# A fused sparse-attention, Fourier-mixing and MLP kernel whose step list is issued in another order on all five engines

## The chip, the cores and the metric

The kernel runs on one NeuronCore of a Trainium2 chip. The metric is device time in microseconds (us) of one execution. Three runs of the kernel before gave 300.67, 300.26 and 299.35 us, a median of 300.26. The profile is of one execution, whose span from its first to its last instruction is 297.65 us.

Five engines have a queue of instructions each and start them strictly in the order of that queue: TensorE (PE, matrix multiplies; its weight loads are shown as PEld), VectorE (DVE), ScalarE (ACT), GpSimd (POOL) and SyncE (SP, which only issues transfers). An instruction that needs another engine's result waits on a semaphore, and everything behind it in its own queue waits with it.

## The reference

Four batches of 768 positions, eight heads of 64. Attention keeps, for every query, its own block of 64 keys and the best three earlier blocks by a gate; its output is x (768 x 512 per batch). Then a two-dimensional Fourier transform is added to x, the rows are normalised, and an MLP of width 2048 follows.

```python
k_rep = k.reshape(B, H, n_blocks, block, D).mean(axis=3)
gate_scores = np.einsum('bhsd,bhnd->bhsn', q, k_rep)      # causal blocks only
top_idx = np.argsort(gate_scores, axis=-1)[..., -3:]      # and the query's own block
scores = scale * np.matmul(q, k.transpose(0, 1, 3, 2))    # masked by block and causally
x = softmax(scores) @ v                                   # heads side by side: (B, 768, 512)
u = x + np.real(np.fft.fft(np.fft.fft(x, axis=1), axis=2))
un = (u - mean(u)) / np.sqrt(var(u) + 1e-06)
out = u + np.maximum(un @ w_ch1, 0.0) @ w_ch2
```

## The kernel before

The work is cut into steps of one to 42 instructions. A string, ORDER, lists every step once, and a loop at the end of the kernel calls the steps in that order. Each engine gets its instructions in exactly this order; no scheduler moves anything. What an instruction must wait for is worked out from the order too: it waits for whatever it reads, and for earlier readers of what it overwrites. Two rules of that bookkeeping matter here. First, waits are kept by tile, so that a write to one half of a tile waits for an earlier-listed read of the other half. Second, two engines that read the same PSUM tile do so one after the other, in the listed order.

The heads are taken in 16 pairs P, four to a batch b. The steps, by their names in ORDER:

- `Lk`, `Lq`, `Lv`: SP issues the loads of k, q, v of a pair. `tk`, `tq`: six TensorE transposes each (line 289). `ks`: VectorE sums the transposed k by blocks (294), `kh` scales the sums (222). `kc`: ScalarE copies k (305; two instructions on line 308 from pair 7 on). `qc`: q to SBUF (316), `qs`: GpSimd converts it (225).
- `g`: gate scores on TensorE (335, 342). `gt`, `gx`, `gl`, `gm`: VectorE transposes them, finds each row's third best, compares, transposes back (349 to 389). `K`, from pair 7 on: GpSimd puts the mask below the q rows (395, 225), so that the score matmul adds it; before pair 7 the mask is added by matmuls (424).
- `s`: one of six score tiles of a pair (412, 417). `e`: its exponential on ScalarE (434). `d`: GpSimd clears above the diagonal (440). `vc`: v is converted. `v`: 42 matmuls with v (452). `x`: VectorE divides by the row sums (463, 222), which also frees the PSUM tile.
- `fs`, `fd`, `f`: VectorE folds x by the transform's symmetries (222). `y`: first transform, two halves per batch (522, 528); `tr` (VectorE, 541) and `ty` (ScalarE, 535) both read the PSUM tile of a half. `m`: second transform (555, 556); `u`: adds x (569, 575); `xu`: shifts the rows (581); `xt` and `un`: transpose, for batch 0 by TensorE (588, 593), later by DMA (596).
- `bn`, `nv`, `nr`: variance and its root. `W`: GpSimd issues the load of a chunk of w1: hidden tiles 0 to 3, 4 to 9, 10 to 15. `X`: half of w2. `w:b,it`: one hidden tile, eight matmuls (632, 634); `r`: its relu, on VectorE for every fourth tile (642), else on ScalarE (644). `c:b,st,h`: eight matmuls of the second product for rows st, half h of the hidden tiles (659; the last rows in column halves, 651). `o`: VectorE scales c and adds u (671). `od`: SP stores the rows.

PSUM holds four tiles of two banks each. All TensorE results pass through these four, so that a new one waits until an earlier tile has been read for the last time. Two row groups st share one c tile, one bank each:

```python
g = next(x for x in (W2_LAST if b == B - 1 else W2_SETS) if st in x)
if st == g[0] and h == 0:
    c_ps[b, g[0]] = pst([128, len(g), 512], f"c{st}_{b}")
```

with W2_SETS = ((0, 1), (2, 3), (4, 5)) and W2_LAST = ((0, 1), (2, 3), (4,), (5,)). Then `c:0,4,*` and `c:0,5,*` write the two halves of one tile, and `o:0,4` and `o:0,5` read one half each.

Of the kernel before, what the change touches and what calls it, by code (L numbers as in the profile page):

```python
# [117 lines left out]
tk:4 gl:2,1 e:1,2 d:1,3 gm:2 g:3 d:1,4 ks:4 d:1,0 v:0 d:1,5 gt:3 vc:1 kc:4 gx:3 e:1,1 s:2,5 Lv:3
Lq:6 LF:0 Lq:7 Lk:6 Lk:7 LT:0 s:2,3 kh:4 gl:3,0 e:2,5 gl:3,1 s:2,4 e:2,3 d:1,1 x:0 tq:5 qs:4 e:2,4
g:4 d:2,3 gm:3 qc:5 s:2,0 d:2,4 s:2,2 d:1,2 e:2,0 gt:4 d:2,5 tk:5 vc:2 gx:4 e:2,2 s:2,1 ks:5 d:2,0  # L120
Lv:4 Lq:8 Lk:8 s:3,1 e:2,1 v:1 gl:4,0 kh:5 gl:4,1 kc:5 d:2,1 gm:4 d:2,2 s:3,2 x:1 e:3,1 vc:3 g:5
e:3,2 Lv:5 Lc:0 d:3,1 s:3,5 gt:5 s:3,0 fs:0,1 e:3,5 s:3,3 d:3,2 gx:5 e:3,0 s:3,4 fs:1,1 tq:6
gl:5,0 e:3,3 fs:0,0 v:2 gl:5,1 fs:1,0 e:3,4 d:3,3 qc:6 d:3,0 s:4,5 x:2 d:3,4 s:4,4 e:4,5 d:3,5
# [664 lines left out]
```

## Time and profile before

| What | us |
|---|---|
| three runs | 300.67, 300.26, 299.35 |
| median | 300.26 |
| profiled execution, first to last instruction | 297.65 |
| first score tile's exponential starts | 13.38 |
| first W1 tile's first matmul | 60.32 |
| last matmul starts its step | 291.93 |

The page of the profile gives busy time by engine, the span in 40 slices, the chain of work that ended last, and the costliest groups of instructions. Its lines number the kernel before. A group's line reads: line, engine, operation, what it writes and reads with shapes, how many, then busy time in us and mean ns of one, then how long the engine had been idle before them and what ended that. The clock that TensorE was granted stands at 1.00 in the whole execution.

### The profile page before, as it was taken

The page shows a single profiled execution, that of the slowest core. Times are in us where ns is not written, and L with a number is a line of the kernel's source. Part 1 is how long each engine was busy: PE and PEld are TensorE (multiplying, and loading weights), DVE is VectorE, ACT ScalarE, POOL GpSimd, SP SyncE. Part 2 cuts the span into 40 slices and gives each one's busy share as a digit, 9 for nine tenths or more (in the row PEclk, how much of TensorE's full clock was granted, in tenths as well). Part 3 has the DMA queues.
Part 4 walks back from the last instruction along what each step waited for, and adds up shares of the span by engine and source line. Part 5 has one row for each costly group of instructions (what it writes and reads, how often), then busy time and mean ns, then how long its engine had stood idle before and what let it go on. Part 6 is the DMA issues. An engine that isn't in the chain of part 4 may idle for free.

```text
...
## 1 busy us (share of the span) xinstructions
PE 285.7 (96%) x2633; PEld 179.1 (60%) x2633; DVE 189.2 (64%) x604; ACT 164.8 (55%) x207; POOL 111.0 (37%) x286
## 2 busy tenths in 40 slices
PE   7798999999999999999999999999999999999994
...
GB/s 170 216 204 220 237 228 202 200 212 206 209 195 214 213 58 174 119 168 178 1 2 2 0 1 143 37 72 70 3 0 2 35 97 47 141 0 2 0 94 121
DMA packets 92768, 33.45 MB, mean 112 GB/s; under 512 B 85504, under 2 KB 89536, under 8 KB 92736
## 3 DMA queue, kind: packets, MB, share of 16 engines
...
q10 hardware_dynamic: 1712, 0.40, 0.7%
...
HBM read 28.55 MB, written 6.29 MB: 117 GB/s over the span
## 4 chain that ended last, share of the span: by engine, by line
PE 79%; DMA 6%; SPq 4%; ACT 4%; issue 3%; POOL 2%; DVE 1%; ACTq 0%; DVEq 0%; POOLq 0%
PE c L659 26%; PE h L632 19%; PE h L634 9%; PE sc L417 7%; PE av L452 5%; PE tp L289 4%; SPq L272 4%; DMA w<-in_moe_w_ch_dram 3%; ACT pt L434 3%; PE yp L522 2%; DMA nat<-in_q_dram 2%; PE mx L556 1%; PE mx L555 1%; PE g L342 1%; PE c L651 1%
## 5 line engine op out<-in xcount | busy, mean ns | idle before, releaser
L434 ACT ACTIVATE pt<-sc 128x1024 f16<-128x1024 f32 (+1 forms) x96 | 83.2, 925 | 25.7 <-PE sc L417 19.5
L632 PE MATMUL h<-unT,w 128*128 128x512 f16 x256 | 85.1, 379 | 0.4 <-DMA w<-in_moe_w_ch_dram 0.4
L659 PE MATMUL c<-w_sb,hT 128*128 128x512 f16 x368 | 83.8, 379 | 0.0
L634 PE MATMUL h<-unT,w 128*128 128x256 f16 x256 | 69.7, 272 | 0.1
L644 ACT ACTIVATE hT<-h 128x768 f16<-128x768 f32 x48 | 37.8, 813 | 44.2 <-PE h L634 44.1
L659 PEld LDWEIGHTS <-hT 128*128 128x128 f16 x368 | 35.6, 98 | 39.3 <-issue 0.5
L440 POOL TENSOR_SCALAR_AFFINE_SELECT pt<-pt 128x256 f16<-128x256 f16 x96 | 37.3, 411 | 54.7 <-ACT pt L434 53.7
L632 PEld LDWEIGHTS <-w 128*128 128x128 f16 x256 | 24.9, 97 | 29.1 <-issue 0.7
L671 DVE SCALAR_TENSOR_TENSOR u<-c,rs,u 128x512 f32<-128x512 f32 (+1 forms) x25 | 17.6, 726 | 31.2 <-PE c L659 30.4
L642 DVE TENSOR_SCALAR hT<-h 128x768 f16<-128x768 f32 x16 | 15.3, 954 | 30.2 <-PE h L634 30.2
L289 PE MATMUL tp<-id,nat 128*128 128x128 f32 x192 | 26.8, 278 | 4.3 <-DVE lt L380 1.0
L581 ACT ACTIVATE x<-u,nm 128x512 f16<-128x512 f32 x24 | 15.9, 715 | 22.4 <-DVE nm L575 22.3
L634 PEld LDWEIGHTS <-w 128*128 128x128 f16 x256 | 25.0, 98 | 4.7 <-DMA unT<-x 0.5
L289 PEld LDWEIGHTS tp<-id,nat 128*128 128x128 f32 x192 | 21.4, 142 | 9.7 <-issue 2.5
L225 POOL TENSOR_SCALAR_AFFINE_SELECT qk<-mt 32x160 f16<-32x160 f16 x72 | 23.1, 341 | 10.7 <-DVE mt L389 9.1
L417 PE MATMUL sc<-qk 96*128 96x512 f16 (+3 forms) x144 | 26.9, 305 | 0.0
L225 POOL TENSOR_SCALAR_AFFINE_SELECT qk<-q 64x768 f16<-64x768 f32 (+1 forms) x25 | 20.6, 824 | 15.2 <-DVE q L316 8.9
L294 DVE TENSOR_REDUCE kr<-tp 128x12 f32<-128x768 f32 x16 | 15.2, 950 | 12.7 <-PE tp L289 12.2
L452 PE MATMUL av<-v,pt 128*128 128x65 f16 x672 | 23.0, 193 | 0.1
L452 PEld LDWEIGHTS <-pt 128*128 128x128 f16 x672 | 22.0, 97 | 1.7 <-issue 0.6
L417 PEld LDWEIGHTS <-qk 96*128 96x128 f16 x144 | 13.4, 97 | 8.9 <-issue 0.7
L222 POOL TENSOR_TENSOR t<-vr,rs 128x6 f32<-128x6 f32 x12 | 2.4, 198 | 43.5 <-DVE rs L612 42.9
...
## 6 DMA issues: line engine op xcount, KB each, us to landing
...
```

Of the source, the lines that this page charges most:

```text
L225: nc.gpsimd.affine_select(out=out, in_=in_, pattern=[[0, i] for i in n], base=0, channel_multiplier=0, compare_op=ALU.is_ge, fill=0.0)
L289: nc.tensor.transpose(ps[:, 128 * st:128 * st + 128], src[:, st, :], id32)
L417: nc.tensor.matmul(ps[:, e, co:co + q1 - q0], qk[0:96, e, 1, 128 * jt:128 * jt + 128], qk[0:96, e, 0, q0:q1], start=True, stop=True)
L434: nc.scalar.activation(out=d["pt"][:, o:o + 2 * n].rearrange("p (e c) -> p e c", e=2), in_=d["sc", i][:, :, 0:n], func=AF.Exp, scale=0.125)
L440: nc.gpsimd.affine_select(out=dg, in_=dg, pattern=[[0, 2], [1, 128]], base=0, channel_multiplier=-1, compare_op=ALU.is_ge, fill=0.0)
L452: nc.tensor.matmul(av[:, e, 66 * st:66 * st + 65], pt[:, co:co + 128], vv[:, e, jt, 0:65], start=(cnt == 0), stop=(cnt == 20))
L581: nc.scalar.activation(out=x_b[:, 2 * kp + k2, :], in_=u_b[:, k2, :], func=AF.Identity, scale=0.0625, bias=nm[:, k2:k2 + 1])
L632: nc.tensor.matmul(hp[:, 0:512], w1s, unT[:, dt, 0:512], start=(dt == 0), stop=(dt == NDT - 1))
L634: nc.tensor.matmul(hp[:, 512:768], w1s, unT[:, dt, 512:768], start=(dt == 0), stop=(dt == NDT - 1))
L644: nc.scalar.activation(out=hT, in_=hp, func=AF.Relu)
L659: nc.tensor.matmul(c_ps[b, g[0]][:, st - g[0], :], h_t[b, it][:, 128 * st:128 * (st + 1)], w2_sb[:, it, :], start=(it == 0), stop=(it == N ...
L671: nc.vector.scalar_tensor_tensor(out=o, in0=ps, scalar=st_t[b][1][:, st:st + 1], in1=o, op0=ALU.mult, op1=ALU.add)
```

## The change

Only the string ORDER differs. It lists the same 1011 steps, and all steps from the first pair on stand in another order. The opening loads of pair 0 and the constants are as before. In the changed file the kernel's lines stand two higher, since the string is two lines shorter. Before, the first W1 tiles of batch 0 are 4, 5, 6, 7 and 3; after, they are 1, 3, 6, 5, 4 and 7. The stretches that matter below, before (-) and after (+), whole lines of the string:

```diff
-Lk:1 Lq:1 Lk:2 Lq:2 tk:0 ks:0 tq:0 Lq:3 Lk:3 kh:0 qc:0 iz:1 tk:1 qs:0 kc:0 g:0 ks:1 iz:0 gt:0 tq:1
-kc:1 gx:0 Lq:4 Lv:0 Lk:4 Lv:1 kh:1 gl:0,0 tk:2 gl:0,1 gm:0 kc:2 qc:1 s:0,3 s:0,2 ks:2 e:0,3 qs:1
...
-tk:7 f:0,3 e:4,2 f:0,0 y:0,1 ks:7 pg:0 W:0 kc:6 y:0,0 tr:0,1 d:4,0 kc:7 d:4,4 d:4,5 ks:6 d:5,5
-d:4,1 ty:0,1 tr:0,0 s:5,3 d:5,2 s:5,4 d:4,3 kh:6 W:1 ty:0,0 m:0,2 qs:6 e:5,3 u:0,2 m:0,1 vc:4
...
-e:6,3 g:7 w:0,0 d:6,5 gt:7 r:0,2 d:6,3 vc:6 gx:7 s:6,4 r:0,0 vc:5 s:6,0 e:6,4 tk:9 Li:0 gl:7,0
-Lv:7 tq:9 gl:7,1 e:6,0 gm:7 w:0,11 Lq:12 Lv:8 K:7 qc:9 kc:9 g:8 r:0,11 v:5 gt:8 d:6,0 ks:9 w:0,8
-qs:9 gx:8 w:0,10 x:5 r:0,8 d:6,4 d:6,2 gl:8,0 s:7,5 s:7,2 r:0,10 kh:9 fs:4,1 w:0,1 bn:0,5 e:7,5
...
-c:0,0,0 tr:1,1 ty:1,1 s:9,5 c:0,2,1 e:9,5 d:8,0 d:9,3 tk:11 K:10 s:8,5 c:0,1,0 Lk:14 ks:11 kc:11
-c:0,3,1 f:1,1 d:9,5 e:8,5 d:9,1 qs:10 tq:12 o:0,2 y:1,0 od:0,2 kh:11 d:8,4 o:0,3 pg:1 vc:10 qc:12
-c:0,1,1 od:0,3 ty:1,0 d:9,4 Lv:12 Lv:13 qs:11 tr:1,0 g:11 c:0,0,1 gt:11 d:8,3 d:8,5 gx:11 qs:12
-m:1,0 o:0,0 m:1,1 od:0,0 o:0,1 d:9,2 od:0,1 v:8 u:1,1 m:1,2 u:1,0 xu:1,1 c:0,4,0 gl:11,0 xu:1,0
...
-qc:13 vc:13 bn:1,4 s:11,2 d:10,5 x:9 s:11,4 vc:12 e:11,2 c:0,5,1 bn:1,1 Lv:14 Lv:15 e:11,4 s:11,0
-o:0,5 s:11,5 w:1,11 e:11,5 od:0,5 o:0,4 e:11,0 kh:12 bn:1,5 od:0,4 s:11,3 w:1,7 e:11,3 r:1,11
...
+tk:0 ks:0 Lq:1 kh:0 tq:0 qc:0 qs:0 g:0 gt:0 gx:0 tq:1 qc:1 qs:1 gl:0,0 gl:0,1 gm:0 Lk:2 tk:2 ks:2
+Lk:1 tk:1 ks:1 kh:1 kc:0 iz:0 kc:2 iz:1 s:0,5 e:0,5 kc:1 Lq:2 s:0,3 s:0,1 e:0,1 tq:2 qc:2 g:1 gt:1
...
+f:0,2 f:0,3 f:0,0 f:0,1 pg:0 W:0 s:5,4 e:5,4 s:4,3 e:4,3 d:4,3 s:5,3 e:5,3 Lk:7 tk:7 y:0,1 tr:0,1
+ks:7 ty:0,1 kc:7 y:0,0 ty:0,0 tr:0,0 Lk:6 s:5,2 tk:6 ks:6 e:5,2 kc:6 m:0,2 u:0,2 W:1 d:5,2 s:5,1
...
+d:5,4 d:5,3 qs:7 kh:7 qc:8 qs:8 W:2 d:5,5 w:0,1 w:0,3 gx:6 r:0,1 w:0,6 kc:8 r:0,6 w:0,5 r:0,5 w:0,4
+r:0,4 w:0,7 ks:8 gl:6,0 gl:6,1 r:0,3 bn:0,1 gm:6 s:6,5 e:6,5 r:0,7 kh:8 s:6,0 e:6,0 s:6,3 g:7 gt:7
+gx:7 fs:4,0 e:6,3 s:6,2 s:6,4 e:6,2 s:6,1 e:6,1 w:0,0 r:0,0 e:6,4 w:0,2 r:0,2 Lc:0 Lv:5 Lv:6 vc:6
+d:6,0 Lk:9 tk:9 kc:9 ks:9 gl:7,0 gl:7,1 g:8 gt:8 gm:7 w:0,11 r:0,11 gx:8 vc:5 v:5 x:5 kh:9 w:0,14
+r:0,14 d:6,1 K:7 X:0 Lq:9 tq:9 s:7,2 e:7,2 Lv:7 s:7,0 qc:9 d:7,2 qs:9 gl:8,0 gl:8,1 bn:0,3 vc:7
...
+m:1,0 u:1,0 xu:1,0 tq:11 qc:11 qs:11 tq:12 s:9,2 e:9,2 c:0,0,1 qc:12 v:8 x:8 g:11 gt:11 o:0,0 s:10,0
+e:10,0 c:0,1,1 s:10,5 s:10,2 e:10,5 e:10,2 Lv:12 un:1,0 od:0,0 Lv:13 gx:11 gl:11,0 gl:11,1 fs:8,0
...
+s:10,3 e:10,3 m:1,2 c:0,5,0 u:1,2 bn:1,1 xu:1,2 K:11 s:11,1 e:11,1 s:11,3 s:11,2 e:11,2 e:11,3
+c:0,4,1 s:10,1 e:10,1 tk:12 kc:12 tq:13 tk:13 kc:13 qc:13 ks:12 bn:1,4 ks:13 kh:12 o:0,4 c:0,5,1
+o:0,5 un:1,2 un:1,1 w:1,5 s:11,0 e:11,0 Lq:15 r:1,5 w:1,14 s:11,4 g:12 gt:12 gx:12 gl:12,0 gl:12,1
...
+y:2,0 ty:2,0 e:13,5 tr:2,0 nv:1 d:13,1 nr:1 d:12,5 d:13,0 vc:13 d:12,2 d:13,4 s:12,4 e:12,4 c:1,0,0
+f:2,3 y:2,1 tr:2,1 ty:2,1 c:1,0,1 o:1,0 Lv:15 Lk:15 tk:15 Lk:14 kc:15 ks:15 tk:14 ks:14 kc:14 kh:15
+kh:14 m:2,1 c:1,1,0 u:2,1 s:13,2 g:14 tq:15 qc:15 e:13,2 d:13,2 c:1,1,1 o:1,1 m:2,2 gt:14 gx:14
...
+c:2,0,1 fd:15,1 fd:15,0 f:3,3 f:3,2 y:3,1 f:3,1 f:3,0 pg:3 y:3,0 tr:3,1 tr:3,0 c:2,1,1 o:2,0 ty:3,1
+ty:3,0 m:3,0 o:2,1 u:3,0 od:2,1 od:1,5 od:2,0 xu:3,0 un:3,0 m:3,1 u:3,1 c:2,4,0 c:2,2,1 o:2,2 od:2,2
...
+w:3,8 r:3,3 r:3,8 r:3,0 w:3,7 r:3,7 w:3,4 r:3,4 nr:3 w:3,6 r:3,6 c:3,2,0 c:3,4,0 c:3,0,0 c:3,1,0
+c:3,1,1 c:3,3,0 o:3,1 c:3,3,1 o:3,3 c:3,2,1 c:3,0,1 o:3,2 od:3,2 od:3,1 od:2,3 c:3,4,1 o:3,4 od:3,3
+od:3,4 od:2,5 o:3,0 od:3,0 c:3,5,1 o:3,6 od:3,6 c:3,5,0 o:3,5 od:3,5
```

In the built program of the new order, the first matmul of `c:0,1,1`, `c:0,5,1`, `c:1,1,0`, `c:1,5,1`, `c:2,3,0` and `c:3,2,1` each carries a wait for VectorE's `o` of the other half of its tile, which now stands ahead of it; in the old order every `c` of a tile stands ahead of that tile's first `o`, and no such wait exists.

More of the change, by code (lines that the diff above doesn't have):

```diff
@@ L118 @@
[L118 to L123, printed above, removed]
@@ new lines @@
+un:2,2 od:1,0 xu:2,1 un:2,1 Lv:14 gt:15 gl:14,1 gm:14 K:14 c:1,4,1 m:2,0 x:13 gx:15 u:2,0 xu:2,0
+gl:15,0 gl:15,1 qs:15 c:1,5,0 v:12 x:12 gm:15 o:1,4 K:15 c:1,2,0 c:1,3,0 s:14,5 e:14,5 c:1,5,1 pg:2
+s:15,5 e:15,5 s:14,3 e:14,3 o:1,5 bn:2,2 bn:2,1 c:1,2,1 s:15,3 s:14,0 e:14,0 e:15,3 s:14,1 e:14,1
+c:1,3,1 s:14,4 e:14,4 od:1,4 un:2,0 w:2,7 r:2,7 fs:12,0 s:15,0 w:2,3 e:15,0 d:15,0 d:14,0 o:1,3
+o:1,2 od:1,2 od:1,3 w:2,15 r:2,15 r:2,3 s:15,1 w:2,5 e:15,1 r:2,5 w:2,11 r:2,11 s:15,2 s:15,4 e:15,4
+e:15,2 w:2,4 s:14,2 e:14,2 d:15,5 d:14,5 d:14,1 d:15,2 vc:14 vc:15 d:15,3 d:14,3 d:14,2 d:15,4
```

83 lines of the change are left out of this document (36 added, 47 removed).

## The prediction

> **What bounds the kernel now.** I read the page's busy times and slices first, then the two stages in a view of windows that starts and ends at events: the first transpose (5.12), the first W1 tile (60.32), the last matmul (293.67).
>
> ```profile
> PE 285.7 (96%) x2633; PEld 179.1 (60%) x2633; DVE 189.2 (64%) x604; ACT 164.8 (55%) x207; POOL 111.0 (37%) x286
> PE   7798999999999999999999999999999999999994
> ```
>
> ```profile
> 5.12:60.32 55.20, 48.63 (x741) 35.78 (x740) 48.00 (x159) 46.26 (x59) 27.45 (x54) 1.00 1.15 215
> 60.32:293.67 233.35, 233.23 (x1884) 141.91 (x1884) 139.34 (x436) 117.04 (x146) 81.85 (x216) 1.00 0.40 86
> ```
>
> The columns are length, then busy TensorE, weight loads, VectorE, ScalarE, GpSimd, the granted clock, the DMA share. From 60.32 on TensorE is busy for 233.23 of 233.35 us at clock 1.00: nothing can be won there, and each microsecond for which a new order makes TensorE wait is added to the end. Up to 60.32 three engines share the load (48.6, 48.0, 46.3 of 55.2), and an order could win or lose. So I went through the new order looking for places where TensorE's own work between two points is shorter than the chain on other engines between the same points. TensorE's prices, from the chain of waits (start, duration, what):
>
> ```profile
> 50.29 9.98 DMA w<-in_moe_w_ch_dram
> ...
> 83.93 0.41 PE g L342 x8
> ...
> 95.84 0.22 PE h L632
> 97.14 0.44 PE sc L417 x4
> 97.58 1.73 PE c L659 x8
> ...
> 107.80 0.66 PE tp L289 x6
> ...
> 119.92 1.28 PE av L452 x42
> ...
> 283.27 1.75 PE c L651 x16
> ```
>
> A step `c` takes 1.73, `v` 1.28, `tk` or `tq` 0.66, `g` 0.41, a score tile 0.44; `w` takes 1.30 (from 95.84 to 97.14); `m`, eight matmuls of 256 columns like the sixteen on line 651, 0.87. The other engines' prices, from the groups kept apart by shape (mean ns of one behind the comma):
>
> ```profile
> L434 ACT ACTIVATE pt<-sc 128x1024 f16<-128x1024 f32 x80 | 78.4, 1032 | 18.6 <-PE sc L417 17.1 <-PE sc L424 1.0
> L644 ACT ACTIVATE hT<-h 128x768 f16<-128x768 f32 x48 | 37.8, 813 | 44.2 <-PE h L634 44.1
> L581 ACT ACTIVATE x<-u,nm 128x512 f16<-128x512 f32 x24 | 15.9, 715 | 22.4 <-DVE nm L575 22.3
> L308 ACT CAST qk<-tp 64x768 f16<-64x768 f32 x18 | 14.3, 792 | 3.2 <-DVE kr L294 3.1
> L535 ACT CAST ty<-yp 128x772 f16<-128x772 f32 x8 | 8.3, 1036 | 4.7 <-PE yp L522 2.7 <-DVE tr L541 1.9
> ```
>
> ```profile
> L671 DVE SCALAR_TENSOR_TENSOR u<-c,rs,u 128x512 f32<-128x512 f32 x23 | 16.6, 747 | 30.5 <-PE c L659 30.4
> L569 DVE SCALAR_TENSOR_TENSOR u<-mx,x 128x512 f32<-128x512 f32 x24 | 15.6, 687 | 3.7 <-PE mx L556 3.6
> L222 DVE TENSOR_TENSOR x<-av,rcp 128x768 f16<-128x768 f32 x16 | 15.3, 958 | 0.6
> L294 DVE TENSOR_REDUCE kr<-tp 128x12 f32<-128x768 f32 x16 | 15.2, 950 | 12.7 <-PE tp L289 12.2 <-ACT qk L305 0.5
> L222 DVE TENSOR_TENSOR fg<-zw 128x762 f16<-128x762 f16 x16 | 8.8, 557 | 0.1
> L541 DVE CAST tr<-yp 128x768 f16<-128x768 f32 x8 | 8.0, 1011 | 6.0 <-PE yp L522 5.6 <-ACT ty L535 0.4
> L463 DVE RECIPROCAL rcp<-av 128x12 f32<-128x12 f32 x16 | 3.5, 218 | 5.8 <-PE av L452 5.7
> L353 DVE STREAM_TRANSPOSE gt<-g 128x160 f32<-128x160 f32 x9 | 3.1, 346 | 3.5 <-PE g L342 3.4
> L389 DVE STREAM_TRANSPOSE mt<-ltb 128x160 f16<-128x160 f16 x9 | 3.1, 343 | 0.2
> L222 DVE TENSOR_TENSOR ltb<-gt,mx 128x120 f16<-128x120 f32 x9 | 2.8, 312 | 0.1
> L575 DVE TENSOR_SCALAR nm<-sm 128x2 f32<-128x2 f32 x12 | 2.2, 181 | 0.6
> L610 DVE TENSOR_SCALAR rs<-vr 128x6 int32<-128x6 int32 x4 | 1.3, 336 | 0.1
> ```
>
> ```profile
> L225 POOL TENSOR_SCALAR_AFFINE_SELECT qk<-mt 32x160 f16<-32x160 f16 x72 | 23.1, 341 | 10.7 <-DVE mt L389 9.1
> ```
>
> The rest comes from the timeline (start, duration, instruction, and in brackets how long the engine had stood idle and for whom):
>
> ```profile
> 42.37 4.72 ACT L434 ACTIVATE pt<-sc 128x1024 f16<-128x1024 f32 x5
> 46.22 1.78 PE L522 MATMUL yp<-fs_sb,fg 128*128 128x193 f16 x19
> 50.34 0.28 PE L555 MATMUL mx<-fd_sb,tr 128*128 128x256 f16 x1
> 58.27 0.68 DVE L593 COPY unT<-xt 128x1024 f16<-128x1024 f16 x1
> 60.32 0.39 PE L632 MATMUL h<-unT,w 128*128 128x512 f16 x1 [0.37 <-DMA w<-in_moe_w_ch_dram]
> 109.54 1.61 ACT L308 CAST qk<-tp 64x768 f16<-64x768 f32 x2 [2.94 <-DVE kr L294]
> 115.31 1.02 DVE L541 CAST tr<-yp 128x768 f16<-128x768 f32 x1 [0.41 <-ACT ty L535]
> ```
>
> The first row says that exponentials in a run cost 0.92 each (five in 4.72, the last in full). The last two show the rule that decides most below: ScalarE's copy of k stood idle for VectorE's sum over the same transposes, and `tr` for `ty`. Readers of one PSUM tile queue up, in either order.
>
> **The change, part by part.** Nothing is removed or added; DMAs, matmuls and copies are the same. So the cost is what TensorE waits for. I allow 0.1 for each hand-over between engines, an estimate: the three rows with an idle time show how long the wait was, not the hand-over itself.
>
> (1) *Up to the first W1 tile, +2.0.* Before, the first `m` starts at 50.34, 3.1 after the first half of `y` ends (46.22 and twelve matmuls, some 1.0). In the new order ScalarE has `ty:0,1`, `kc:7`, `ty:0,0`, and VectorE `tr:0,1`, `ks:7`, `tr:0,0`, each waiting for its fellow reader: tr 1.01, ty 1.04 (ks beside it), kc 1.58, ty 1.04, tr 1.01 make 5.7, with hand-overs 6.1. So `m:0,2` comes 3.0 later, if `y:0,1` comes when it did; ahead of it the engines have the same work in both orders. From `m:0,2` to the last `un` before took 8.6 (50.34 to 58.95); a `kc:6` and a score tile now stand between the `m` steps, +0.3. The first W1 tile would start at 50.34 + 3.0 + 8.9 = 62.3, against 60.32, where the 0.37 of waiting for W1 falls away: chunk 0 is issued first, and chunk 1 has only one GpSimd step ahead of it instead of seven. SP's loads keep nearly their old sequence by pair; fs and fd come earlier. Bounds: -1.5, if the opening (first scores, `ks` before `kc` nearly everywhere) runs 3.5 faster; +4.5, if `ks` before `kc` costs what the 2.94 row shows for ScalarE once more.
>
> (2) *`s:7,2` waits for `K:7`, +2.7.* From the end of `s:6,0` the chain is five exponentials (4.6), two relus (1.6), `kc:9` (1.6), `ks:9` (0.95), which is listed behind it, `gl` 0.3, `gt` 0.35, `gm` 0.35 and some memsets 0.2, `K:7` 8 x 0.341 = 2.7: 12.7, with hand-overs 13.1. TensorE has four score tiles (1.75), two gates (0.8), four `w` (5.2), `tk` and `tq` (1.3) and `v:5` (1.3): 10.4. What the narrow score tiles of line 424 add to a full one I do not know to a few tenths, and a hand-over more or less is the rest: stall 13.1 - 10.4 = 2.7. Bounds 2.0 and 4.1.
>
> (3) *`c:0,1,1` waits for `o:0,0`, +2.1.* From the end of `v:8`: `x:8` 0.22 + 0.96, `gt:11` 0.35 and its memsets 0.15, `o:0,0` 0.75: 2.4, 2.6 with hand-overs; TensorE has `g:11` and one score tile, 0.85: 1.75. Just ahead `s:9,2` waits for `u:1,0` (2 x 0.69 + 0.18 and a hand-over, against two `tq`): 0.35. Bounds 1.5 and 2.8.
>
> (4) *`c:0,5,1` waits for `o:0,4`, +4.8.* From the end of `m:1,2`: `u:1,2` 1.55, `xu:1,2` 1.45, which ScalarE has ahead of four exponentials (3.7), `kc:12` and `kc:13` (3.2), then `ks:13` 0.95, `kh` 0.2, `o:0,4` 0.75: 11.8, 12.1 with hand-overs partly overlapped. TensorE has two `c`, four score tiles and three sets of transposes: 3.46 + 1.75 + 1.98 = 7.2. Bounds 4.0 and 5.5. Behind it stand the first W1 tiles of batch 1; nobody else is delayed.
>
> (5) *`y:2,1` waits for `f:2,3`, +1.4.* `ty` 1.04, `tr` 1.01 behind it, `nv` with three small instructions (about 0.25 each, the longest is line 610), `f` 0.56 and its copy: 3.6; TensorE has `c:1,0,0` and a score tile, 2.2. Bounds 0.9 and 1.8.
>
> (6) *`g:14` waits for `kc:14`, +1.8.* `kc:15` 1.58, `ks:15` 0.95, `ks:14` 0.95, `kc:14` 1.58, with hand-overs 5.5; TensorE has `tk:14`, `m`, `c` and a score tile: 3.7. Bounds 1.2 and 2.2.
>
> (7) *`m:3,0` waits for `ty:3,0`, +0.5* (`tr` and `ty` in turn, 2.3, against one `c`), and *(8) `c:3,2,1` for `o:3,3`, +0.95* (0.75 and two hand-overs, nothing between). Bounds 1.0 and 2.0 together.
>
> The other waits I followed (`c:1,1,0`, `c:1,5,1`, `c:2,3,0`, the DMA transposes, the halves of w2) have a `c` or more between and are hidden by it. The tail has the same last steps: one `o`, one store. Sum: 2.0 + 2.7 + 2.1 + 4.8 + 1.4 + 1.8 + 0.5 + 0.95 = 16.3. The span becomes 297.65 + 16.3 = 313.9. The median of the runs lies 300.26 - 297.65 = 2.6 above the span, so I predict 316.5.
>
> A rule speaks against (3), (4) and (8): in the Trainium skill, "PSUM — Partial Sum Buffer", section "PSUM bank collisions raise a hardware error", it is one bank that two engines must not touch at once, and the two halves of a `c` tile are two banks. By it these waits would not be needed and the sum would be 8.8, the time 309. No row of before can show it; the built program has the waits, so I keep them, and take the other case as a rival.
>
> **The rivals.** *The halves do not hold each other up*: terms (3), (4), (8) shrink to the 0.35 of `u:1,0`: 316.5 - 7.5 = 309. For it speaks that before never shows such a wait; against it, the program's waits.
>
> *TensorE's clock falls during the long waits.*
>
> ```profile
> L696 PE MATMUL warmps<-zeros 128*128 128x512 f16 x9 | 4.0, 631 | 1.3 <-DVE half L697 1.3
> ```
>
> At the start nine 512-column matmuls take 4.0, 0.44 each, twice a `c`'s 0.216. If each of the three long waits, (1), (2) and (4), were followed by 4 us at that rate, 2 us would be lost each time: 322.5. Against it speaks the granted clock of 1.00 in every window, through gaps of about 1 us. The Trainium skill, "TensorE: Matmul & The Clock Gate", section "Why this matters for your kernels", wants no gap over some 3 us; only (4) is clearly longer, and by that page one place and 318.5 would be likely.
>
> *Faster*: the stage up to 60.32 is packed better. Its place is VectorE's queue, busy 48.0 of 55.2: at most 7.2 can go, and the first W1 tile would start at 53. For it speak the start with chunk 0 and VectorE's prefix, equal in both orders. The time is 300.3 - 7.2 = 293 if (2) to (8) are all hidden as well; it decides as soon as that gain exceeds what is left of them, 14.3 by my sum. Against it: TensorE cannot save after 60.32.
>
> *The order does nothing*: the eight waits are covered and the start is equal, 300.
>
> **How the numbers follow.** The forecast, 310 to 322, gets 0.62; the halves that do not wait 0.12; the clock 0.10; faster 0.07; no difference 0.03; over 327, through waits that I overlooked, 0.06. Bounds of the terms together: -1.5 + 2.0 + 1.5 + 4.0 + 0.9 + 1.2 + 1.0 = 9.1 and 4.5 + 4.1 + 2.8 + 5.5 + 1.8 + 2.2 + 2.0 = 22.9, so 309 to 323; towards both rivals I go to 306 and 325. Within 0.5% of 300.26, about what a measurement can tell from no change, 0.03; slower 0.90.
>
> **What would show it.** In the changed profile TensorE should have one long idle time on line 657 for VectorE's line 669, near 5 us, and shorter ones for the mask copies ahead of pair 7's scores, for line 495 to 505 or `tr` ahead of `y` of batch 2 and for the copies of k ahead of a gate of pair 14; the first W1 tile should start at 62; busy TensorE from there should stay at some 233 in a stretch 14 longer. I am wrong if that stretch is not longer, if those idle times are absent, or if the first W1 tile is earlier than 58.

## The result, and the profile after

The changed kernel takes 320.12 us (median of four runs, 319.93 to 321.9), the kernel before on the same chip 300.40: a ratio of 1.068 (95% interval 1.064 to 1.071). The profiled execution has a span of 317.71.

From the page, the busy times and the slices of the changed kernel (tenths of busy time; the second slice line is the clock that TensorE was granted):

```profile
PE 292.4 (92%) x2633; PEld 181.4 (57%) x2633; DVE 186.3 (59%) x604; ACT 164.9 (52%) x207; POOL 113.9 (36%) x286
PE   7589996999799998994999998999999999999985
PEclk9999999899999999997899999999999999999999
```

The windows of the changed kernel, cut at the same events as before (first transpose, first W1 tile, last matmul), with the columns as before:

```profile
5.12:65.14 60.02, 50.36 (x741) 36.99 (x740) 45.88 (x159) 44.98 (x57) 25.95 (x52) 0.97 1.05 196
65.14:314.07 248.93, 238.23 (x1886) 142.98 (x1883) 138.58 (x436) 118.38 (x148) 86.25 (x218) 0.99 0.39 82
```

The start is 4.82 longer than before (60.02 against 55.20), the stretch behind it 15.58 (248.93 against 233.35); 0.34 comes back after the last matmul. In that second stretch TensorE now stands idle for 10.70, against 0.12, and its busy time grew by 5.00 for the same matmuls: a clock below 1.00 is in there.

The start up to the first matmul of `y:0,1` (47.48 after, 46.22 before), first the changed kernel, then the kernel before:

```profile
5.12:47.48 42.36, 35.92 (x572) 25.51 (x571) 32.86 (x125) 33.55 (x43) 17.86 (x35) 1.00 1.10 209
5.12:46.22 41.10, 35.93 (x577) 25.59 (x576) 34.36 (x129) 34.02 (x44) 17.48 (x34) 1.00 1.16 220
```

TensorE is busy for the same time in both, so the 1.26 by which `y:0,1` comes later are idle time.

What TensorE waited for, in the changed kernel's view of waits (engine, line, released by; us in total, times, longest):

```profile
PE c L657 <- DVE u L669: 6.4, 3, 4.0
PE mx L553 <- DVE tr L539: 2.7, 1, 2.7
PE sc L422 <- ACT indz L711: 1.8, 1, 1.8
PE sc L415 <- POOL qk L223: 1.6, 1, 1.6
PE g L340 <- DVE nm L573: 1.5, 1, 1.5
...
PE yp L520 <- DVE fg L505: 0.5, 1, 0.5
PE mx L553 <- ACT ty L533: 0.4, 1, 0.4
```

The first row is three steps `c` that wait for VectorE's `o` (line 669). The places, from the timeline of TensorE (start, duration, instruction, in brackets the idle time and who ended it):

```profile
47.48 1.78 PE L520 MATMUL yp<-fs_sb,fg 128*128 128x193 f16 x19
...
54.39 0.40 PE L553 MATMUL mx<-fd_sb,tr 128*128 128x256 f16 x1 [2.68 <-DVE tr L539]
...
65.14 0.38 PE L630 MATMUL h<-unT,w 128*128 128x512 f16 x1
...
86.05 1.11 PE L415 MATMUL sc<-qk 96*128 96x512 f16 x4 [1.62 <-POOL qk L223]
...
127.78 1.89 PE L657 MATMUL c<-w_sb,hT 128*128 128x512 f16 x8 [1.43 <-DVE u L669]
...
147.36 3.57 PE L657 MATMUL c<-w_sb,hT 128*128 128x512 f16 x8 [4.02 <-DVE u L669]
...
185.39 0.67 PE L520 MATMUL yp<-fs_sb,fg 128*128 128x193 f16 x6
186.59 0.68 PE L520 MATMUL yp<-fs_sb,fg 128*128 128x193 f16 x6 [0.52 <-DVE fg L505]
...
194.83 0.48 PE L340 MATMUL g<-q,krb 128*32 128x160 f32 x8 [1.49 <-DVE nm L573]
...
256.56 0.28 PE L553 MATMUL mx<-fd_sb,ty 128*128 128x256 f16 x1 [0.44 <-ACT ty L533]
...
305.24 2.97 PE L657 MATMUL c<-w_sb,hT 128*128 128x512 f16 x13 [0.91 <-DVE u L669]
```

The rows with an idle time are the steps `m:0,2`, `s:7,2`, `c:0,1,1`, `c:0,5,1`, `y:2,1`, `g:14`, `m:3,0` and `c:3,2,1`: the eight places of the forecast. The first row, without one, is `y:0,1`, and the one at 65.14 is the first W1 tile. `c:0,5,1` at 147.36 took 3.57 for eight matmuls that take 1.89 at 127.78. Windows of the changed kernel around the two longest waits (the number after GpSimd's is the granted clock):

```profile
50.70:54.20 3.50, 0.88 (x6) 0.64 (x6) 0.88 (x1) 3.43 (x5) 0.28 (x1) 1.00 1.14 178
54.20:57.60 3.40, 3.21 (x23) 1.99 (x24) 2.25 (x6) 1.17 (x2) 0.40 (x1) 0.50 1.19 218
57.60:61.00 3.40, 3.39 (x37) 2.59 (x35) 2.81 (x12) 2.90 (x5) 2.68 (x7) 1.00 0.68 125
143.00:146.40 3.40, 0.34 (x4) 0.17 (x2) 2.94 (x5) 2.47 (x4) 0.00 (x0) 1.00 0.70 156
146.40:149.80 3.40, 2.44 (x6) 0.84 (x6) 0.90 (x3) 0.00 (x0) 0.00 (x0) 0.50 0.61 119
149.80:153.20 3.40, 3.40 (x11) 1.45 (x10) 0.75 (x1) 0.00 (x0) 0.00 (x0) 0.50 0.18 67
153.20:156.60 3.40, 3.40 (x27) 1.68 (x26) 0.45 (x5) 1.73 (x2) 1.56 (x3) 1.00 0.44 164
```

Behind the first wait the clock is halved for 3.4 us, behind the second for 6.8.

### The profile page after: what moved, and what is told of

It is laid out like the page before. It is cut to its first block, busy times and chain, and to the rows that moved or that the text cites. A ratio compares the mean times of both kernels' runs of the same rounds, so it can differ in the third digit from the quotient of the medians.

```text
span 317.7 us, 6730 instructions
## 1 busy us (share of the span) xinstructions
PE 292.4 (92%) x2633; PEld 181.4 (57%) x2633; DVE 186.3 (59%) x604; ACT 164.9 (52%) x207; POOL 113.9 (36%) x286
## 4 chain that ended last, share of the span: by engine, by line
PE 67%; DVE 17%; ACT 9%; DMA 2%; POOL 2%; issue 1%; SPq 0%; ACTq 0%; DVEq 0%
PE c L657 20%; PE h L630 17%; PE h L632 8%; PE sc L415 6%; PE av L450 4%; ACT pt L432 3%; PE tp L287 3%; DVE u L567 3%; DVE kr L292 2%; ACT qk L306 2%; PE yp L520 2%; DMA nat<-in_q_dram 2%; POOL qk L223 2%; DVE x L220 2%; PE mx L553 1%
## 5 line engine op out<-in xcount | busy, mean ns | idle before, releaser
L657 PE MATMUL c<-w_sb,hT 128*128 128x512 f16 x368 | 85.8, 384 | 6.4 <-DVE u L669 6.4
L669 DVE SCALAR_TENSOR_TENSOR u<-c,rs,u 128x512 f32<-128x512 f32 (+1 forms) x25 | 17.8, 723 | 32.0 <-PE c L657 29.2
L223 POOL TENSOR_SCALAR_AFFINE_SELECT qk<-mt 32x160 f16<-32x160 f16 x72 | 22.9, 339 | 16.3 <-DVE mt L387 11.5
L223 POOL TENSOR_SCALAR_AFFINE_SELECT qk<-q 64x768 f16<-64x768 f32 (+1 forms) x25 | 20.7, 827 | 11.8 <-ACT q L312 6.1
L220 POOL TENSOR_TENSOR t<-vr,rs 128x6 f32<-128x6 f32 x12 | 3.5, 292 | 55.6 <-DVE rs L610 55.0
L567 DVE SCALAR_TENSOR_TENSOR u<-mx,x 128x512 f32<-128x512 f32 x24 | 15.6, 689 | 8.6 <-PE mx L554 5.3
```

The costliest lines, as they stand in the source:

```text
L223: nc.gpsimd.affine_select(out=out, in_=in_, pattern=[[0, i] for i in n], base=0, channel_multiplier=0, compare_op=ALU.is_ge, fill=0.0)
L567: nc.vector.scalar_tensor_tensor(out=u_b[:, k2, :].rearrange("p (m two) -> p two m", two=2), in0=mps[:, k2, :].rearrange("p (two m) -> p t ...
L657: nc.tensor.matmul(c_ps[b, g[0]][:, st - g[0], :], h_t[b, it][:, 128 * st:128 * (st + 1)], w2_sb[:, it, :], start=(it == 0), stop=(it == N ...
```

## The experiments

Each run is compared with the kernel before, run on the same chip beside it (median 299.75 to 300.25); "loss" is a median less the median of before. The changed kernel's loss is 19.7.

**One half-tile wait taken out.**

```diff
-c:0,4,1 s:10,1 e:10,1 tk:12 kc:12 tq:13 tk:13 kc:13 qc:13 ks:12 bn:1,4 ks:13 kh:12 o:0,4 c:0,5,1
+c:0,4,1 s:10,1 e:10,1 tk:12 kc:12 tq:13 tk:13 kc:13 qc:13 ks:12 bn:1,4 ks:13 kh:12 c:0,5,1 o:0,4
```

> The changed kernel with o:0,4 listed behind c:0,5,1 instead of ahead of it. Theory A (the 4.02 us that TensorE stood idle ahead of c:0,5,1 were the wait for o:0,4, and the half clock behind them, worth 2.9 us, came from that idle time): both go, 320.1 - 4.0 - 2.9 = 313.2. Theory B (the wait is real, but the low clock behind it has another cause): 316. Theory C (other engines are late anyway, and the wait moves on to w:1,5 and the score tiles of pair 11): 318 to 320, with a new idle time of 2 us or more within ten steps.

Measured: 313.94, loss 13.7. TensorE's timeline of this run:

```profile
141.79 2.02 PE L287 MATMUL tp<-id,nat 128*128 128x128 f32 x14
143.65 1.89 PE L657 MATMUL c<-w_sb,hT 128*128 128x512 f16 x8
145.38 0.38 PE L630 MATMUL h<-unT,w 128*128 128x512 f16 x1
```

`c:0,5,1` follows the transposes at once, at full clock, and no new idle time appears in the steps behind it. Theory A holds, with 6.0 of the expected 6.9; B and C fall. In this trace the half clock behind `m:0,2` lasts 6.8 us, against 3.4 in the changed kernel's, so the gain is not read clean of it.

**The first Fourier stage.**

```diff
-ks:7 ty:0,1 kc:7 y:0,0 ty:0,0 tr:0,0 Lk:6 s:5,2 tk:6 ks:6 e:5,2 kc:6 m:0,2 u:0,2 W:1 d:5,2 s:5,1
+ty:0,1 y:0,0 tr:0,0 ty:0,0 ks:7 kc:7 Lk:6 s:5,2 tk:6 ks:6 e:5,2 kc:6 m:0,2 u:0,2 W:1 d:5,2 s:5,1
```

> The changed kernel with ks:7 and kc:7 listed behind tr:0,0 and ty:0,0, and tr:0,0 ahead of ty:0,0, so that the four readers of the first transform's halves go side by side. Theory A (the 2.68 us ahead of m:0,2 came from readers in turn with kc:7 between, and the low clock behind it, some 0.9 us, from the idle time): 320.1 - 2.5 - 0.9 = 316.7, the first W1 tile some 3.4 earlier, at 61.7. Theory B (tk:6 and the score tiles now wait for the PSUM tile that tk:7 holds longer): 318.5 to 320, with an idle time of 1.5 or more ahead of tk:6 or s:5,2.

Measured: 319.66, loss 19.4, a gain of 0.3: by the median inside B's range. But the trace shows something else. TensorE at `m:0,2`, and windows of the opening of this run:

```profile
54.75 0.27 PE L553 MATMUL mx<-fd_sb,tr 128*128 128x256 f16 x1 [0.65 <-ACT ty L533]
```

```profile
10.40:13.80 3.40, 1.62 (x16) 1.10 (x14) 3.27 (x11) 0.51 (x1) 0.82 (x1) 1.00 1.35 218
13.80:20.60 6.80, 5.73 (x52) 3.33 (x52) 2.62 (x14) 4.41 (x7) 0.81 (x2) 0.50 1.35 220
```

The wait shrank from 2.68 to 0.65, and `tk:6` and `s:5,2` do not wait, so B's reason is absent; the matmuls of `m:0,2` are at full clock again. From `y:0,1` to the first W1 tile it takes 15.79 (49.88 to 65.67) against 17.66 in the changed kernel: 1.9 of the 3.4 that A expected, as waits of 0.42, 0.39 and 0.69 follow (ahead of `s:5,1`, `m:0,1` and `xt`), where the changed kernel has one of 0.31. But in this execution the clock was halved from 13.8 to 20.6, in the opening that both kernels share, and `y:0,1` came 2.4 later than in the changed kernel's trace. The mean clocks of the four runs were 0.978, 0.978, 0.984 and 0.987, at 320.45, 320.54, 318.87 and 318.10. The mechanism stands, with 1.9 in the trace; its size by the median isn't told by this run.

**Four other waits.**

```diff
-d:6,0 Lk:9 tk:9 kc:9 ks:9 gl:7,0 gl:7,1 g:8 gt:8 gm:7 w:0,11 r:0,11 gx:8 vc:5 v:5 x:5 kh:9 w:0,14
+d:6,0 Lk:9 tk:9 kc:9 gl:7,0 gl:7,1 gm:7 ks:9 g:8 gt:8 w:0,11 r:0,11 gx:8 vc:5 v:5 x:5 kh:9 w:0,14
...
-y:2,0 ty:2,0 e:13,5 tr:2,0 nv:1 d:13,1 nr:1 d:12,5 d:13,0 vc:13 d:12,2 d:13,4 s:12,4 e:12,4 c:1,0,0
-f:2,3 y:2,1 tr:2,1 ty:2,1 c:1,0,1 o:1,0 Lv:15 Lk:15 tk:15 Lk:14 kc:15 ks:15 tk:14 ks:14 kc:14 kh:15
-kh:14 m:2,1 c:1,1,0 u:2,1 s:13,2 g:14 tq:15 qc:15 e:13,2 d:13,2 c:1,1,1 o:1,1 m:2,2 gt:14 gx:14
+y:2,0 ty:2,0 e:13,5 tr:2,0 f:2,3 nv:1 d:13,1 nr:1 d:12,5 d:13,0 vc:13 d:12,2 d:13,4 s:12,4 e:12,4 c:1,0,0
+y:2,1 tr:2,1 ty:2,1 c:1,0,1 o:1,0 Lv:15 Lk:15 tk:15 Lk:14 kc:15 ks:15 tk:14 ks:14 kc:14 kh:15
+kh:14 m:2,1 c:1,1,0 u:2,1 s:13,2 tq:15 qc:15 e:13,2 d:13,2 c:1,1,1 g:14 o:1,1 m:2,2 gt:14 gx:14
...
-ty:3,0 m:3,0 o:2,1 u:3,0 od:2,1 od:1,5 od:2,0 xu:3,0 un:3,0 m:3,1 u:3,1 c:2,4,0 c:2,2,1 o:2,2 od:2,2
+ty:3,0 c:2,2,1 m:3,0 o:2,1 u:3,0 od:2,1 od:1,5 od:2,0 xu:3,0 un:3,0 m:3,1 u:3,1 c:2,4,0 o:2,2 od:2,2
```

> The changed kernel with four places mended that hold no half-tile wait: gm:7 ahead of ks:9, f:2,3 ahead of nv:1, g:14 behind c:1,1,1, c:2,2,1 ahead of m:3,0. Theory A (each is a wait of its own): the idle times ahead of s:7,2 (1.62), y:2,1 (0.52), g:14 (1.49) and m:3,0 (0.44) go, 4.1 in all, less 0.3 for what is left of them: 320.1 - 3.8 = 316.3. Theory C (waits move on, as the engines behind are late by the same work): 318.5 to 320.

Measured: 317.89, loss 17.6, a gain of 2.1, half of what A expected. The waits ahead of `s:7,2`, `y:2,1` and `m:3,0` are gone from the view of waits; two new rows stand there:

```profile
PE tp L287 <- DVE nm L573: 1.3, 1, 1.3
...
PE h L632 <- DMA unT<-x: 0.6, 1, 0.6
```

The first is `tq:15`, which had been listed behind `g:14` and now stands where it stood: it needs a PSUM tile, and the four are held until `kc:14` and `u:2,1` have read theirs (1.3 of the 1.49). The second is `w:3,1`, which waits for its transposed rows. So two of the four gave their time, and of the two others most moved one step on: C is right for those.

**All mended together**, with `o:0,0` and `o:3,3` moved behind `c:0,1,1` and `c:3,2,1` and the two fillings of zeros moved up:

```diff
-Lk:1 tk:1 ks:1 kh:1 kc:0 iz:0 kc:2 iz:1 s:0,5 e:0,5 kc:1 Lq:2 s:0,3 s:0,1 e:0,1 tq:2 qc:2 g:1 gt:1
+Lk:1 tk:1 ks:1 kh:1 iz:0 iz:1 kc:0 kc:2 s:0,5 e:0,5 kc:1 Lq:2 s:0,3 s:0,1 e:0,1 tq:2 qc:2 g:1 gt:1
```

> The changed kernel with all of this: the three runs above, o:0,0 behind c:0,1,1, o:3,3 behind c:3,2,1, and the two fillings of zeros iz:0 and iz:1 ahead of kc:0 at the start. Theory A (the loss is a sum of separate waits with two falls of the clock): 320.1 less 6.9, 3.4, 3.8, 1.6 for c:0,1,1, 1.0 for c:3,2,1 and 0.8 for the start = 302.6, at a granted clock of 1.00. Theory C (the new order carries a loss of its own that moves from one place to the next): 308 or more.

Measured: 305.99, loss 5.7. Seven tenths of the loss are gone by moving 13 of 1011 steps, but 3.4 more is left than the sum said. Windows of this run:

```profile
5.20:8.60 3.40, 1.68 (x13) 1.21 (x11) 1.14 (x2) 0.89 (x2) 0.00 (x0) 1.00 1.36 216
8.60:12.00 3.40, 3.28 (x18) 2.36 (x19) 1.85 (x12) 2.33 (x4) 0.83 (x1) 0.51 1.35 217
...
62.94:300.55 237.61, 234.69 (x1886) 141.91 (x1883) 138.04 (x436) 118.27 (x148) 85.79 (x218) 1.00 0.40 86
```

The first W1 tile starts at 62.94, still 2.6 late, with 3.4 us of half clock in the opening of this execution; the stretch behind it, to the last matmul, is 4.3 longer than in the kernel before instead of 15.6.

**Start and rest apart.** Two mixed lists. In the first stand the steps of the old order up to the first `w`, then those that are left in the new order with its mends. At the seam it reads:

```
un:0,1 kc:8 xt:0,0 qc:8 tq:7 un:0,0 qs:8 v:4 Lq:10 Lk:10 Lv:6 Lq:11 qc:7 bn:0,3 x:4 d:5,3 qs:7 kh:7
w:0,1 w:0,3 gx:6 r:0,1 w:0,6 r:0,6 w:0,5 r:0,5 w:0,4 r:0,4 w:0,7 ks:8 gl:6,0 gl:6,1 r:0,3 bn:0,1
```

Two places are mended otherwise than above, here against the changed kernel (`f:2,3` stands ahead of `nv:1`, as above):

```diff
-f:2,3 y:2,1 tr:2,1 ty:2,1 c:1,0,1 o:1,0 Lv:15 Lk:15 tk:15 Lk:14 kc:15 ks:15 tk:14 ks:14 kc:14 kh:15
+y:2,1 tr:2,1 ty:2,1 c:1,0,1 o:1,0 Lv:15 Lk:15 tk:15 Lk:14 kc:15 tk:14 ks:14 ks:15 kc:14 kh:15
...
-c:2,0,1 fd:15,1 fd:15,0 f:3,3 f:3,2 y:3,1 f:3,1 f:3,0 pg:3 y:3,0 tr:3,1 tr:3,0 c:2,1,1 o:2,0 ty:3,1
-ty:3,0 m:3,0 o:2,1 u:3,0 od:2,1 od:1,5 od:2,0 xu:3,0 un:3,0 m:3,1 u:3,1 c:2,4,0 c:2,2,1 o:2,2 od:2,2
+c:2,0,1 fd:15,1 fd:15,0 f:3,3 f:3,2 y:3,1 f:3,1 f:3,0 pg:3 y:3,0 tr:3,1 ty:3,0 tr:3,0 c:2,1,1 o:2,0 ty:3,1
+m:3,0 o:2,1 u:3,0 od:2,1 od:1,5 od:2,0 xu:3,0 un:3,0 m:3,1 u:3,1 c:2,4,0 c:2,2,1 o:2,2 od:2,2
```

> All steps up to the first W1 tile as in the kernel before, then the new order with all its places mended, and two of the mends made anew: at pair 14, ks:14 ahead of ks:15 in place of moving g:14, and at batch 3, ty:3,0 ahead of tr:3,0 in place of moving c:2,2,1. Theory A (start and rest each carry their own loss): the first W1 tile starts at 60.3 again, and of the rest only the 0.8 ahead of m:1,2 and some small waits are left: 300.3 + 1.4 = 301.7. Theory C (a loss that moves on): 304 or more, with idle times of over 1 us that the run with all mended did not have.

Measured: 303.74, loss 4.0, between the two theories. Windows, ScalarE and TensorE of this run:

```profile
5.12:59.68 54.56, 48.11 (x741) 35.38 (x739) 47.37 (x159) 46.25 (x59) 27.12 (x53) 1.00 1.15 217
59.68:296.77 237.09, 235.05 (x1890) 142.08 (x1886) 137.22 (x437) 116.67 (x146) 84.88 (x217) 1.00 0.40 86
```

```profile
176.74 1.60 ACT L307 CAST qk<-tp 64x768 f16<-64x768 f32 x2 [0.79 <-DVE kr L293]
```

```profile
178.39 0.48 PE L341 MATMUL g<-q,krb 128*32 128x160 f32 x8 [0.16 <-ACT qk L307]
179.25 0.84 PE L288 MATMUL tp<-id,nat 128*128 128x128 f32 x6 [0.38 <-DVE u L568]
```

The start is the old one again, and behind it no idle time over 0.8 is left, as A said. `kc:14` ends at 178.34 and `g:14` starts at 178.39: it was the copy of k that held `g:14`, although the changed kernel's row names another VectorE instruction, `u:2,1`, which there ended within 0.03 of `kc:14`. But the rest is still 3.7 longer than the old one (237.09 against 233.35), in small pieces: 2.0 idle, and 1.8 of busy time beyond the old 233.23, at a clock of 1.00.

The reverse, the new start and then the steps that are left in the old order; at the seam:

```
d:5,4 d:5,3 qs:7 kh:7 qc:8 qs:8 W:2 d:5,5 Lv:5 Lc:0 Lk:9 Lq:9 kc:8 Lq:10 Lk:10 Lv:6 Lq:11 bn:0,3
w:0,4 bn:0,1 w:0,5 r:0,4 gx:6 ks:8 w:0,6 r:0,5 gl:6,0 gl:6,1 w:0,7 r:0,6 gm:6 w:0,3 r:0,7 s:6,5
```

> All steps up to the first W1 tile in the changed kernel's order, unmended, and then the steps that are left in the order of the kernel before. Theory A (the start costs the 4.8 us by which its first W1 tile comes later, and the old rest keeps TensorE fed): 300.3 + 4.8 = 305.1, and up to 1.7 more if the clock falls once more in the opening. Rival (a late start leaves the other engines ahead, and the rest wins some of it back): 303 or less.

Measured: 306.12, loss 6.4, as A with its addition for the clock, which in this trace stands at half from 53.4 to 60.3, for 6.8 us instead of 3.4. Windows:

```profile
5.12:66.02 60.90, 51.32 (x741) 37.32 (x740) 46.96 (x159) 46.44 (x59) 25.99 (x52) 0.94 1.07 204
66.02:299.95 233.93, 233.18 (x1886) 141.89 (x1883) 139.96 (x436) 117.04 (x146) 83.80 (x218) 1.00 0.40 84
```

The old rest behind the late start takes 233.93 against 233.35: nothing is won back.

**The half-tile wait put into the old order.**

```diff
-qc:13 vc:13 bn:1,4 s:11,2 d:10,5 x:9 s:11,4 vc:12 e:11,2 c:0,5,1 bn:1,1 Lv:14 Lv:15 e:11,4 s:11,0
-o:0,5 s:11,5 w:1,11 e:11,5 od:0,5 o:0,4 e:11,0 kh:12 bn:1,5 od:0,4 s:11,3 w:1,7 e:11,3 r:1,11
+qc:13 vc:13 bn:1,4 s:11,2 d:10,5 x:9 s:11,4 vc:12 e:11,2 o:0,4 c:0,5,1 bn:1,1 Lv:14 Lv:15 e:11,4 s:11,0
+o:0,5 s:11,5 w:1,11 e:11,5 od:0,5 e:11,0 kh:12 bn:1,5 od:0,4 s:11,3 w:1,7 e:11,3 r:1,11
```

> The kernel before with one step moved: o:0,4 stands ahead of c:0,5,1. In its trace VectorE ends x:9 at 132.13, o:0,4 takes 0.75, and c:0,5,1 started at 131.57. Theory A (a read of one half of the tile holds up the write of the other): c:0,5,1 starts at 133.0, an idle time of 1.4 ahead of it, the clock stays at 1.00: 300.3 + 1.4 = 301.7. Rival (halves do not hold each other, the wait ahead of c:0,5,1 in the changed kernel has another cause): 300.3, no idle time.

Measured: 300.45, a ratio of 1.0021 (1.0011 to 1.0032). VectorE and TensorE of this run:

```profile
131.76 0.74 DVE L671 SCALAR_TENSOR_TENSOR u<-c,rs,u 128x512 f32<-128x512 f32 x1
```

```profile
132.55 1.89 PE L659 MATMUL c<-w_sb,hT 128*128 128x512 f16 x8 [1.11 <-DVE u L671]
```

`c:0,5,1` starts 0.05 after the end of the read of the other half, after 1.11 of idle time: the halves do hold each other. The time grew by 0.6 us (0.0021 of 300) and not by 1.1, as `w:1,11` behind it, which took 1.76 in the old order, now takes 1.47 like its neighbours, and the start of this execution was 0.24 shorter.

**The first chunk of w1 first**, alone, in the old order: 0 to 3 and 4 to 7 change places in `w` and `r` of batch 0.

```diff
-w:0,4 d:5,3 qs:7 bn:0,1 w:0,5 r:0,4 gx:6 ks:8 w:0,6 r:0,5 gl:6,0 kh:7 gl:6,1 x:4 w:0,7 r:0,6 gm:6
+w:0,0 d:5,3 qs:7 bn:0,1 w:0,1 r:0,0 gx:6 ks:8 w:0,2 r:0,1 gl:6,0 kh:7 gl:6,1 x:4 w:0,3 r:0,2 gm:6
```

> The kernel before with hidden tiles 0 to 3 of batch 0 in the places of 4 to 7 and the other way round, w and r alike, so that the first W1 tiles read the first chunk of w1. Theory A: only the 0.37 us of waiting for the second chunk goes: 299.9, inside what can be told from no change. Rival (the chunk is worth more, as the first tiles could start earlier): under 299.

Measured: a ratio of 0.9982 (0.9955 to 1.0009), no difference. The first W1 tile starts at 59.76, 0.56 earlier, and the view of waits has a row that before has not, `w:1,11` waiting for its rows:

```profile
PE h L634 <- DMA unT<-x: 0.4, 1, 0.4
```

**The long wait filled.** The wait for `o:0,4` stays, but TensorE has eleven extra matmuls in it, whose result is not used:

```diff
-c:0,4,1 s:10,1 e:10,1 tk:12 kc:12 tq:13 tk:13 kc:13 qc:13 ks:12 bn:1,4 ks:13 kh:12 o:0,4 c:0,5,1
+c:0,4,1 s:10,1 e:10,1 tk:12 kc:12 tq:13 tk:13 kc:13 qc:13 ks:12 bn:1,4 ks:13 kh:12 o:0,4 wm:11 c:0,5,1
...
+    def warm(n):
+        wps = pst([128, 512], "warm")
+        for _ in range(n):
+            nc.tensor.matmul(wps, id16, w2_sb[:, 0, :], start=True, stop=True)
+        nc.scalar.copy(out=dummy, in_=wps[:, 0:1])
```

> The changed kernel with eleven extra matmuls of 512 columns (2.4 us at 0.216 each) into a PSUM tile of their own, listed between o:0,4 and c:0,5,1, and one copy of a column of it by ScalarE; the order of all else is as in the changed kernel. c:0,5,1 still waits for o:0,4, but TensorE is no longer idle for 4 us. Theory A (the half clock behind c:0,5,1 comes from TensorE being busy for less than about half of some 3.4 us): no low clock around c:0,5,1, 320.1 - 2.9 = 317.2. Rival (the low clock has another cause, such as what the transfers or the other engines do there): c:0,5,1 still takes 3.57, 320.

Measured: 317.93, loss 17.8, a gain of 1.9 by doing more work. TensorE of this run:

```profile
146.06 2.53 PE L663 MATMUL warm<-w_sb,id 128*128 128x512 f16 x11 [0.20 <-DVE q L314]
149.86 1.89 PE L657 MATMUL c<-w_sb,hT 128*128 128x512 f16 x8 [1.27 <-DVE u L675]
```

Same wait, same neighbours, and `c:0,5,1` takes 1.89 instead of 3.57: the low clock came from TensorE's idleness.

**A long wait in the old order.**

```diff
-qc:13 vc:13 bn:1,4 s:11,2 d:10,5 x:9 s:11,4 vc:12 e:11,2 c:0,5,1 bn:1,1 Lv:14 Lv:15 e:11,4 s:11,0
-o:0,5 s:11,5 w:1,11 e:11,5 od:0,5 o:0,4 e:11,0 kh:12 bn:1,5 od:0,4 s:11,3 w:1,7 e:11,3 r:1,11
+qc:13 vc:13 bn:1,4 s:11,2 d:10,5 x:9 s:11,4 vc:12 e:11,2 bn:1,1 bn:1,5 o:0,4 c:0,5,1 Lv:14 Lv:15 e:11,4 s:11,0
+o:0,5 s:11,5 w:1,11 e:11,5 od:0,5 e:11,0 kh:12 od:0,4 s:11,3 w:1,7 e:11,3 r:1,11
```

> The kernel before with bn:1,1, bn:1,5 and o:0,4 moved ahead of c:0,5,1: the wait of the run with o:0,4 alone (1.11) and two times 0.9 more on VectorE, 2.9 us of idle TensorE in the middle of its stretch of solid work. Theory A (TensorE's clock is halved when it was busy for less than about half of some 3.4 us, for 3.4 or 6.8 us): 299.75 + 2.6 + 1.7 = 304.0, up to 305.7, with a granted clock of 0.50 for 3 to 7 us behind c:0,5,1. Rival (only idle times of over 3.4 us halve it): 302.4 at clock 1.00.

Measured: 303.33, a ratio of 1.0100 (1.0086 to 1.0114). TensorE of the profiled execution:

```profile
134.87 1.89 PE L659 MATMUL c<-w_sb,hT 128*128 128x512 f16 x8 [2.70 <-DVE u L671]
```

Here 2.70 of idle time left the clock alone: this execution had a mean clock of 1.00 and took 302.47, as the rival has it. The four others had 0.993 or 0.994 and took 303.05 to 303.68: 0.006 of 301 us is 1.8 us, one stretch of 3.4 at half clock. The kernel before, beside them, stands at 0.997 to 1.00. So the same wait seems to halve the clock in some executions and not in others; the place of the fall is not shown, as only one execution has a trace. The 0.6 to 1.2 us that these four took longer are about what the kernel before varies by itself (299.46 to 300.55).

**Chunk 0 first, and the next wait filled**, in the old order: `w:1,11` goes behind `s:11,3`.

```diff
-o:0,5 s:11,5 w:1,11 e:11,5 od:0,5 o:0,4 e:11,0 kh:12 bn:1,5 od:0,4 s:11,3 w:1,7 e:11,3 r:1,11
+o:0,5 s:11,5 e:11,5 od:0,5 o:0,4 e:11,0 kh:12 bn:1,5 od:0,4 s:11,3 w:1,11 w:1,7 e:11,3 r:1,11
```

> The kernel before with the hidden tiles of chunk 0 first, as in an earlier run, and w:1,11 moved behind s:11,3, so that the 0.41 us for which it waited there is filled. Theory A (TensorE's waits are all that the order can change): 299.7 - 0.4 = 299.3 or 0.2 to 0.3% under the kernel before, at the edge of what five rounds tell. Rival (the wait moves on to the next steps): no difference.

Measured: 299.30, a ratio of 0.9961 (0.9947 to 0.9976). It is the one version here whose interval lies under the kernel before, by 0.4%. Its trace does not show A's reason: the wait of `h` for its rows is 0.2 instead of 0.4, and a new wait of 0.4 for GpSimd (line 225) stands ahead of a score tile, as the rival has it.

## Why the prediction was right or wrong

The time, 320.12, lies inside the range and 3.6 above the forecast of 316.5; the direction and the eight places are right, and the places that the forecast held to be hidden (`c:1,1,0`, `c:1,5,1`, `c:2,3,0`, the transposes by DMA, the halves of w2) show no wait. By the steps of the forecast:

| Step | forecast | measured in the trace |
|---|---|---|
| (1) first W1 tile | 62.3, +2.0 | 65.14, +4.8, half clock in it |
| (2) `s:7,2` | 2.7 | 1.62 |
| (3) `c:0,1,1` | 2.1 | 1.43 |
| (4) `c:0,5,1` | 4.8 | 4.02, and 2.9 of clock |
| (5) `y:2,1` | 1.4 | 0.52 |
| (6) `g:14` | 1.8 | 1.49 |
| (7) `m:3,0` | 0.5 | 0.44 |
| (8) `c:3,2,1` | 0.95 | 0.91 |
| (2) to (8) | 14.25 | 10.43, and 2.9 of clock |

- **The waits (2) to (8)** were sized too long by 3.8 together, 2.7 of it in (2), (4) and (5). In (2) the chain took 12.4 and not 13.1 (from the end of `s:6,0` at 73.67 to 86.05), and TensorE's own work 10.8 and not 10.4 (to 84.43). The hand-overs that the working added, 0.4, are not there; the durations without them, 12.7, were 0.3 too long, and the rest is TensorE's work. In (4) it is the same, 11.5 and not 12.1 (11.8 without hand-overs) from the end of `m:1,2` (135.84), against 7.5 of work and not 7.2. In (3) the 0.35 ahead of `s:9,2` did not come. In (5) a cover was overlooked: `y:2,1` issues its first six matmuls, which read other parts of the folded rows, before the one that waits for `f:2,3`, 0.67 us of work in the row at 185.39.
- **The start** was sized too short by 2.8. From `y:0,1` to `m:0,2` the forecast said 3.0 more and the trace shows 2.8 (6.91 against 4.12): the readers in turn, with `kc:7` between, were sized well. What failed is the sentence that `y:0,1` comes when it did: it starts at 47.48 against 46.22, and the forecast put that at nothing because the engines have the same work ahead of it. They nearly have (only `tk:6` now comes behind), but in another order: TensorE's busy time up to there is the same (35.92 against 35.93), and its idle time is 1.26 longer. The longest of its waits that are new are 1.8 for the filling of the zeros, 1.0 for a copy of k and 0.9 for the copy of q; waits of 1.0 and 0.8 for VectorE's gate steps, ahead of transposes, are gone. How the 1.26 divides among them was not separated: with the zeros mended `y:0,1` still came at 47.15, in an execution with half clock there. And from `m:0,2` to the first W1 tile it takes 10.75 against 9.98, 0.8 more, and not 8.9 as the forecast had it: it counted to the last `un`, but `v:4` and `tq:8` stand between, and TensorE worked for 3.2 us of it at half clock (the eight matmuls of `m:0,2` took 1.68 against 0.90).
- **The clock**, a rival with a chance of 0.10, came in at two of its three places: half of the busy time at half clock is 1.6 behind (1), part of which other waits may cover, and 2.9 behind (4), at most 4.5 us together, where the rival had 6. The filled wait and the run without that wait show that TensorE's idleness is the cause at (4). A gap of 2.68 was enough at (1); 1.62 at (2) was not. The rule of the Trainium skill that the prediction names ("TensorE: Matmul & The Clock Gate", section "Why this matters for your kernels", no gap over some 3 us) gave one place and 2 us; the trace has a second place, with a gap under 3 us.
- **The halves that do not hold each other**, the other rival with a price, is refuted by the old order with `o:0,4` moved up (1.11 us of waiting, the read being in the other bank) and by the changed order with it moved back. By the rule of the Trainium skill in "PSUM — Partial Sum Buffer", section "PSUM bank collisions raise a hardware error", the banks would not need it, and no run here tests that; the time is decided by the program's bookkeeping by tile.
- **The sum** reads 16.3 forecast and 20.06 measured in the span (317.71 - 297.65). That is 4.8 for the start and 15.6 for the rest, less 0.3 at the end; the 15.6 are 10.6 more idle time, 2.9 of clock and 2.1 of other busy time, a term that the forecast has not: it held that busy TensorE would stay at some 233, and it is 238.23. In these 2.1 a single matmul takes no longer (a 512-column score matmul 379 ns in the mean of both kernels, a transpose 275 against 274); they start a little further apart, which counts as busy, most in the transposes (10.5 us for 86 records in the trace against 9.3 for 84, each counted up to the next start). What spaces them is not shown. So the number was near partly by luck: waits sized too long (3.8) stood against a start sized too short (2.8), the clock and this spacing.
- **Faster** and **no difference** fall. The windows show why the first did: the new start leaves TensorE 9.7 us idle of 60.0 where the old left it 6.6 of 55.2, although VectorE has 2.1 less to do in it.
